# Two attention-and-MLP layers on one core: the last four x tiles of layer 0 turned through device memory, and the k/q weight stores moved behind the loop

## The chip, the core and the metric

The kernel runs on 1 core of a Trainium2 chip. The metric is the device time of one execution in microseconds (us). The kernel before has a median of 1320.75 us in 3 runs (1319.97 to 1321.23).

## What is computed

Two layers are applied to `x` (2048 rows, 640 columns, fp32). Each layer is a linear attention block followed by a squared-ReLU MLP, each with a layer norm ahead of it and a residual around it. Both layers use the same weights.

```python
def _A_ref(x, wqkv, wo):                     # H = 32 heads of Dh = 20
    q, k, v = split_heads(x @ wqkv)
    phi = lambda t: where(t > 0, t + 1, exp(t)) + 1e-6
    pq, pk = phi(q), phi(k)
    kv = einsum("bhsd,bhse->bhde", pk, v)
    z  = einsum("bhsd->bhd", pk)
    o  = einsum("bhqd,bhde->bhqe", pq, kv) / (einsum("bhqd,bhd->bhq", pq, z)[..., None] + 1e-6)
    return merge_heads(o) @ wo

def _B_ref(x, w1, b1, w2, b2):               # F = 1728
    r = maximum(x @ w1 + b1, 0)
    return (r * r) @ w2 + b2

x = x + _A_ref(layernorm(x), wqkv, wo)       # these two lines
x = x + _B_ref(layernorm(x), w1, b1, w2, b2) # are done twice
```

## The kernel before

**Arithmetic.** Every fp32 product is made of three matmuls of a rounded kind: an operand is split into a high part (a ScalarE copy) and a low part (a VectorE subtraction), and the products low-high, high-low and high-high are added up. Each operand that TensorE reads therefore costs one ScalarE copy and one VectorE subtraction.

**Stages of a layer.** First the attention loop over 16 tiles of 128 rows: `part` (line 489 in the profile) projects a tile onto k and q, `Phi` (lines 591, 598, 599) makes exp, min and max of it, and `g_part`/`gt_part` (line 489 too) add up the products of phi(k) with the normalised x. Then a transition (lines 990 to 1170: `late_q`, `kv_make`, `m_make`, `b_out`), which folds v and the output weights into one 640x640 matrix M and finishes the first four tiles of the attention. Then the MLP over four groups of four tiles (lines 1204 and 1287), with the attention's output of the next group woven in (line 489).

**The order of the work** is written out by hand; no scheduler moves an instruction. Each engine runs its own instructions in that order, and stops where an operand is not ready. All loads and stores but two kinds are issued by SyncE's queue (SP), in order too; a DMA there also waits until the one eight places before it has landed. GpSimd (POOL) issues the accumulating stores of `acc` and the stores of `spread_out`.

**One turn of the attention loop, at tile t** (`late` is the set of tiles whose q part is put off to the transition; 11 to 15 are late in layer 0):

- TensorE: first half of `part(t)`, then, for a late tile, at once the second half, then `g_part(t - 1)` and, at every second tile, `gt_part`.
- ScalarE: `exp` of the first half; the high part of `xh`; a high copy of a weight being prepared (`prep.high`, line 301, layer 0 only); the high part of `xT[t + 1]` (line 502); a further `prep.high`; `exp` of the second half; the high part of `kh` (line 783).
- VectorE: the normalisation of `xt[t + 2]` (`a_apply`, line 389), the rest of phi of the first half (598, 599), `prep.low` (313), the rest of phi of the second half, the low part of `xT[t + 1]` (line 505), that of `xh`, statistics of tile t + 3, the low part of `kh`.

**Turning x.** TensorE needs the normalised tile transposed. Both layers do it without TensorE:

- Layer 0, by block moves: VectorE transposes 32x32 blocks inside the tile (`blocks_x`, line 461, in `x_begin(t + 2)` right behind `a_apply`), then ScalarE moves the 16 blocks to their places (`turn_move`, line 475, issued by `move`, 16 small copies a tile).
- Layer 1, through memory: POOL stores the tile to device memory (`spread_out`, line 417), SP reads it back with the blocks spread in four DMAs (`spread_in`, line 426), both in `x_begin(t + 2)`, and VectorE transposes the blocks (`turn`, line 436) in `x_end(t + 1)`, one turn of the loop later, right ahead of the high copy of `xT[t + 1]`.

```python
def x_begin(t):
    yza[t] = blocks_x(xt[t]) if layer == 0 else spread(xt[t])
def x_end(t):
    return yza.pop(t)[1] if layer == 0 else turn(yza.pop(t), True)
```

**Keeping weights.** Layer 0 prepares the split weights of the MLP during its attention loop (`Prep`: loads, `mix` on POOL, `high`, `low`, `store`, lines 246 to 327) and stores them to device memory. The split k/q weights, five tiles `kq[c]` of two halves, are stored too (`keep_kq`, line 196: 640 KB a half), since layer 1 loads them again. Before the change `keep_kq` stands at the start of the turns t = 11 to 15, two halves a turn.

Of the kernel before, what the change touches and what calls it, by code (L numbers as in the profile page):

```python
# [16 lines left out]
NT = S // P  # L17
DC = D // P
# [25 lines left out]

PREP = {1: "aa", 2: "aa", 3: "t", 4: "aa", 5: "t", 6: "aa", 7: "t", 8: "aa", 9: "t", 10: "aa", 11: "t", 12: "aa"}
LATE_T = (5, 6)
PREP_AT = range(1, 14)
N_WARM = 25

# [16 lines left out]
def kernel(  # L66
# [25 lines left out]
    def bank(i, n=1):  # L92
        return PS[:, 512 * i : 512 * (i + n)]
# [17 lines left out]
    def ftile(name):  # L111
        return tmp.tile([P, D], F32, tag="f", name=name, bufs=F_BUFS)
# [82 lines left out]
    def keep_kq(c, j):  # L195
        nc.sync.dma_start(kept["kq", c][:, j], kq[c][:, j].bitcast(F32))
# [215 lines left out]
    def spread_out(src):  # L412

        n = bounce[0] % 8
        bounce[0] += 1
        d = dram.tile([P, D], F32, name="xb", tag=f"xb_{n}")
        nc.gpsimd.dma_start(d, src)
        return d

    def spread(src):  # L420
        return spread_in(spread_out(src))

    def spread_in(d):
        z = ftile("z")
        for j in range(JQ):
            nc.sync.dma_start(
                z[j * B32 : (j + 1) * B32].rearrange("p (i f) -> p i f", f=Q),
                d[:, j * Q : (j + 1) * Q].rearrange("(i q) f -> q i f", q=B32),
            )
        return z  # L430

    def turn(z, strided=False):

        y = ftile("y")
        order = "p (i q c) -> p i c q" if strided else "p (i c q) -> p i c q"
        nc.vector.transpose(
            out=y.rearrange("p (c i q) -> p i c q", c=DC, q=B32),
            in_=z.rearrange(order, c=DC, q=B32),
        )
        return y  # L440
# [18 lines left out]
    def blocks_x(src):  # L459
        y = ftile("y")  # L460
        nc.vector.transpose(
            out=y.rearrange("p (j c q) -> p j c q", c=DC, q=B32),
            in_=src.rearrange("p (j q c) -> p j c q", c=DC, q=B32),
        )
        return [y]

    def turn_move(yz, js):

        if len(yz) == 1:
            yz.append(ftile("z"))  # L470
        yv = yz[0].rearrange("p (j c q) -> p j c q", c=DC, q=B32)
        zv = yz[1].rearrange("p (c i q) -> p c i q", c=DC, q=B32)
        for j in js:
            for i in range(P // B32):
                nc.scalar.activation(  # L475
                    zv[j * B32 : (j + 1) * B32, :, i, :], yv[i * B32 : (i + 1) * B32, j], AF.Copy
                )
# [33 lines left out]
    def proj(ps, aT, w, cs=range(DC)):  # L511

        for c in cs:
            for k, l in ((1, 0), (0, 0), (0, 1)):
                for j in range(2):
                    nc.tensor.matmul(  # L516
                        ps[:, j * 512 : j * 512 + HD], aT[:, k, c, :], w[c][:, l, j * HD : (j + 1) * HD],
                        start=c == 0 and (k, l) == (1, 0), stop=c == DC - 1 and (k, l) == (0, 1),
                    )
# [6 lines left out]
    xt, xT = {}, {}  # L526
# [21 lines left out]
    for layer in range(N_LAYERS):  # L548
# [21 lines left out]
        def xbank():  # L570
            xbanks.append(xbanks.pop(0))
            return bank(xbanks[-1])

        def part(t, a, b, ps=None):

            ps = (xbank() if ps is None else ps)[:, : b - a]
            for c in range(DC):
                mm3(
                    ps, xT[t][:, 0, c, :], xT[t][:, 1, c, :],
                    kq[c][:, 0, a:b], kq[c][:, 1, a:b], c == 0, c == DC - 1,  # L580
                )
            return ps
# [31 lines left out]
        def g_part(t, i):  # L614

            ps = bank(GB[i])
            a, b = xh[t][:, :, i * P : (i + 1) * P], kh[t][:, :, :DM]
            mm3(ps, a[:, 0], a[:, 1], b[:, 0], b[:, 1], t == 0, t == NT - 1)

        def gt_part(p, j, ps):  # L620

            ps, rs = ps[:, :HD], slice(j * HD, (j + 1) * HD)
            for t in (2 * p, 2 * p + 1):
                a, b = kh[t][:, :, DM:], xh[t][:, :, rs]
                mm3(ps, a[:, 0], a[:, 1], b[:, 0], b[:, 1], t % 2 == 0, t % 2 == 1)
            if p == 0:
                nc.vector.tensor_copy(GT_[:, rs], ps)
            else:
                nc.vector.tensor_tensor(out=GT_[:, rs], in0=ps, in1=GT_[:, rs], op=ALU.add)
# [56 lines left out]
        yza = {}  # L686
# [25 lines left out]
        def x1_at(t):  # L712
            g, i = divmod(t, TG)
            if g % 2 == 0:
                return gtile("x1")
            return x1_odd["tile"][:, i]

        def b_load_x(t):
            xr[t] = x1_at(t)
            nc.sync.dma_start(xr[t], src[t])  # L720
# [73 lines left out]

        moved = {}

        def x_begin(t):
            yza[t] = blocks_x(xt[t]) if layer == 0 else spread(xt[t])

        def x_end(t):  # L800
            return yza.pop(t)[1] if layer == 0 else turn(yza.pop(t), True)

        def move(t, n=JQ):

            if layer == 0 and t in yza:
                turn_move(yza[t], range(moved.get(t, 0), n))
                moved[t] = n

        def prep_step(t, i):
            if layer == 0 and t in PREP_AT:  # L810
                if i == 0:
                    prep.mix()
                    prep.load(PREP.get(t + 1, ""))
                prep.low()
                if (t, i) != (1, 0):
                    prep.high()
                if i % 2 == 0:
                    prep.store(2)
# [4 lines left out]
        for t in range(NT):  # L823
# [5 lines left out]
            if layer == 0:  # L829
                if t >= 14:  # L830
                    prep.store()
                if t >= NT - DC:
                    for j in range(2):
                        keep_kq(t - NT + DC, j)
            if t >= 13:
                b_load_pq(t - 13)
                load_vo(2 * t - 26)
# [130 lines left out]
        def late_q(n=1, rest=True):  # L968

            for _ in range(n):  # L970
                if not late_parts:
                    return
                t, j = late_parts.pop(0)
                if j == 0:
                    late_phi[t] = Phi(ftile("rl"))
                late_phi[t].exp(j * HD, part(t, D + j * HD, D + (j + 1) * HD))
                late_todo.append((t, j))
                if rest:
                    late_rest()
# [3 lines left out]
        def late_rest(n=9):  # L983
            for _ in range(min(n, len(late_todo))):
                t, j = late_todo.pop(0)
                late_phi[t].rest()
                if j == 1:
                    nc.sync.dma_start(pqd[t], late_phi.pop(t).r)

        late_q(2)  # L990
        zbc = tmp.tile([P, D], F32, tag="z", name="zbc", bufs=1)
        psz = [xbank()[:, :HD] for _ in range(2)]
# [5 lines left out]
        for i in range(DC):  # L998
            g_part(NT - 1, i)
            nc.scalar.activation(G[:, i], bank(GB[i]), AF.Copy)  # L1000
        for j in range(2):
            gt_part(NT // 2 - 1, j, xbank())
        b_blocks(0)
# [14 lines left out]
        def run_side(n=1):  # L1018
            for _ in range(min(n, len(side_work))):
                side_work.pop(0)()  # L1020
# [48 lines left out]
        def m_split(m):  # L1069
            nc.vector.tensor_copy(M[m][:, 0], m_raw[m])  # L1070
            nc.vector.tensor_tensor(
                out=M[m][:, 1], in0=m_raw[m], in1=M[m][:, 0].bitcast(F32), op=ALU.subtract
            )
# [50 lines left out]

        po = {}

        for i in range(2):
            po[i] = bank(4 + 2 * i, 2)
            proj(po[i], pT[i], M, range(3))
            if i == 0:  # L1130
                m_split(4)
            run_side(2)

        def x_turned(i):

            b_x1(i, po[i])
            yzx[i] = blocks_T(xn.pop(i))
            side_work.extend(lambda k=k: turn_move(yzx[i], (k,)) for k in range(JQ))
            side_work.append(lambda: f_split(i, yzx.pop(i)[1]))

        for i in range(2):
            proj(po[i], pT.pop(i), M, range(3, DC))
            run_side(1)
            b_load_x(i + 2)
        x_turned(0)
        run_side(2)
        x_turned(1)
# [183 lines left out]
        def at(g, n, f):  # L1331
            events.setdefault((g, n), []).append(f)
# [99 lines left out]
        def prep_last():  # L1432
            x1 = x1_odd["tile"]
            h = [R[:, i, 1].rearrange("p c n -> p (c n)")[:, HT + D * j : HT + D * (j + 1)] for i in range(2) for j in range(2)]
            spots = {5: (x1[:, 2], x1[:, 3], h[0]), 6: (h[1], h[3], h[2])}
            for i, p in enumerate(LATE_T):
                at(0, i, lambda p=p: prep.mixes.append(prep.load_t(p, spots[p])))
                at(0, 1 + 3 * i, prep.mix)
            assert len(LATE_T) == len(prep.t)

# [104 lines left out]
```

## Time and profile before

| | |
|---|---|
| median of 3 runs | 1320.75 us (1319.97 to 1321.23) |
| the profiled execution, its own time | 1320.5 us |
| its span, first to last instruction | 1318.5 us |
| TensorE busy | 1310.7 us, 99% |
| VectorE busy | 865.5 us, 66% |
| ScalarE busy | 735.5 us, 56% |
| GpSimd busy | 219.1 us, 17% |
| attention loop of layer 0, transition | to 194 us, 194 to 255 us |
| attention loop of layer 1 | about 663 to 845 us |
| `turn_move`, all | 272 moves, 334 ns each |
| `kept_kq` stores | 10, 640 KB each |

Times in the views are microseconds from the start of the span. PE is TensorE, DVE is VectorE, ACT is ScalarE, SPq and POOLq are the DMA issues of these queues. A row of a timeline has start, duration, engine, line and operation, output<-input with shapes, and the count of like instructions merged into it; brackets at its end name the idle time before it and what ended it.

### The profile page before, as it was taken

To read this page: it belongs to the slowest core of one execution; us is meant where nothing else is said; L and a number is where in the kernel's file an instruction comes from. 1 tells how busy PE (TensorE), PEld (TensorE's weight loads), DVE (VectorE), ACT (ScalarE), POOL (GpSimd) and SP (SyncE) were. 2 spreads that over 40 slices of the span, in tenths; PEclk is the share of its full clock that TensorE was granted. 3 is DMA by queue.
4 is the path that set the end of the run, shared out by engine and by line. 5 is a ranking of instruction groups with operands and counts; after the bars stand their busy time and mean duration, and the time that the engine had idled before them with its cause. 6 is when DMAs were issued, how large, how long until landed. Compare 5 with 4: busy or idle time off the path is not lost.

```text
span 1318.5 us, 20882 instructions
## 1 busy us (share of the span) xinstructions
PE 1310.7 (99%) x7477; PEld 1193.5 (91%) x7477; DVE 865.5 (66%) x1575; ACT 735.5 (56%) x1594; POOL 219.1 (17%) x289
## 2 busy tenths in 40 slices
PE   9999999999999999999999999999999999999998
PEld 8888889989988988998988889999899899889888
DVE  7888958767944954833856677686577559449045
ACT  5888967785475467334322233387844744854242
POOL 2333310064012002101012222001320120120000
PEclk9999999999999999999999999999999999999999
DMA  6898994499974985898954456454869659749756
GB/s 194 247 278 270 336 339 144 152 353 388 320 290 154 302 298 171 267 361 290 361 158 126 123 145 169 124 199 171 315 214 345 212 192 320 290 149 297 286 186 219
DMA packets 135036, 321.57 MB, mean 244 GB/s; under 512 B 16710, under 2 KB 61894, under 8 KB 134294
## 3 DMA queue, kind: packets, MB, share of 16 engines
q1 hardware_dynamic: 127702, 297.96, 67.1%
q0 software_dynamic: 7232, 22.29, 6.4%
q8 instruction: 59, 0.97, 0.3%
q14 instruction: 43, 0.35, 0.1%
HBM read 242.82 MB, written 65.54 MB: 234 GB/s over the span
## 4 chain that ended last, share of the span: by engine, by line
PE 91%; ACT 2%; DVE 2%; DMA 2%; SPq 1%; issue 1%; POOL 0%; ACTq 0%; DVEq 0%; POOLq 0%
PE PS L489 32%; PE PS L1204 28%; PE PS L1287 25%; PE PS L516 3%; ACT z L475 1%; PE PS L1042 1%; PE PS L1055 1%; DMA kq<-kept_kq 1%; SPq L246 1%; PE PS L849 0%; PE PS L637 0%; DMA xt<-in_A_x_dram 0%; DMA kept<-uprep 0%; DVE xT L505 0%; DVE r L599 0%
## 5 line engine op out<-in xcount | busy, mean ns | idle before, releaser
L1204 PE MATMUL PS<-xTb,u 128*128 128x512 f32 x1640 | 376.6, 389 | 0.0
L1204 PEld LDWEIGHTS PS<-xTb,u 128*128 128x128 f32 x1640 | 306.8, 188 | 62.5
L489 PE MATMUL PS<-kq,xT 128*128 128x320 f32 (+2 forms) x1575 | 285.0, 334 | 1.6 <-DVE xT L505 1.4
L489 PEld LDWEIGHTS PS<-kq,xT 128*128 128x128 f32 x1575 | 250.2, 188 | 29.8 <-DVE xT L505 2.2
L1287 PE MATMUL PS<-u,arena 128*128 128x320 f32 x1644 | 250.2, 309 | 0.0
L1287 PEld LDWEIGHTS PS<-u,arena 128*128 128x128 f32 x1644 | 243.4, 188 | 0.0
L1268 DVE TENSOR_TENSOR arena<-R,arena 128x512 fp32r<-128x512 f32 (+1 forms) x200 | 140.8, 707 | 135.3 <-ACT arena L1259 134.8
L1259 ACT ACTIVATE arena<-R 128x512 fp32r<-128x512 f32 (+1 forms) x200 | 117.9, 593 | 157.9 <-PE PS L1287 131.9
L455 ACT ACTIVATE z<-y 32x160 f32<-32x160 f32 x512 | 171.1, 334 | 49.8 <-DVE y L446 42.2
L1215 ACT ACTIVATE R<-PS,b1sb 128x512 f32<-128x512 f32 x104 | 71.5, 687 | 127.8 <-PE PS L1204 126.9
L489 PE MATMUL PS<-kh,xh 128*128 128x512 f32 x480 | 124.8, 393 | 1.0 <-DVE kh L793 0.9
L383 POOL TENSOR_SCALAR rs<-mv 128x1 f32<-128x1 f32 x64 | 34.9, 546 | 513.8 <-DVE mv L381 513.8
L489 PE MATMUL PS<-uM,pTs 128*128 128x320 f32 x720 | 109.4, 309 | 0.0
L489 PEld LDWEIGHTS PS<-uM,pTs 128*128 128x128 f32 x720 | 107.5, 188 | 1.9
L1287 PE MATMUL PS<-uw,arena 128*128 128x320 f32 x660 | 106.1, 309 | 0.0
L489 PEld LDWEIGHTS PS<-kh,xh 128*128 128x128 f32 x480 | 87.1, 188 | 16.9 <-DVE kh L793 1.8
L1287 PEld LDWEIGHTS PS<-uw,arena 128*128 128x128 f32 x660 | 99.2, 188 | 0.4 <-DVE x L1301 0.2
L1233 DVE TENSOR_TENSOR R<-R 128x512 f32<-128x512 f32 (+1 forms) x128 | 79.5, 626 | 26.0 <-ACT R L1216 26.0
L475 ACT ACTIVATE z<-y 32x160 f32<-32x160 f32 x272 | 90.9, 334 | 3.3
L591 ACT ACTIVATE r<-PS 128x512 f32<-128x512 f32 (+1 forms) x64 | 27.7, 434 | 99.4 <-PE PS L489 98.1
L1216 ACT ACTIVATE R<-R 128x512 f32<-128x512 f32 x104 | 65.8, 633 | 3.3
L598 DVE TENSOR_SCALAR r<-r 128x512 f32<-128x512 f32 (+1 forms) x64 | 21.3, 332 | 70.4 <-ACT r L591 70.2
(135 smaller groups left out, 1318.1 us busy)
## 6 DMA issues: line engine op xcount, KB each, us to landing
u<-kept SPq DMA_DIRECT2D x113, 640.0 KB, 5.6
u<-kept_w SPq DMA_DIRECT2D x104, 640.0 KB, 6.2
u<-kept SPq DMA_DIRECT2D x56, 320.0 KB, 6.1
kept<-uprep SPq DMA_DIRECT2D x49, 320.0 KB, 5.6
z<-xb SPq DMA_DIRECT2D x160, 80.0 KB, 5.3
pqt<-pq SPq DMA_DIRECT2D x32, 320.0 KB, 6.7
acc<-r POOLq DMA_DIRECT2D x28, 320.0 KB, 4.9
uw<-kept SPq DMA_DIRECT2D x14, 640.0 KB, 7.4
```

What stands on the lines that cost most here:

```text
L383: nc.gpsimd.tensor_scalar(rs, mv[:, 1:2], LN_EPS, None, op0=ALU.add)
L455: nc.scalar.activation(zv[j * B32 : (j + 1) * B32, :, i, :], yv[i * B32 : (i + 1) * B32, :, j, :], AF.Copy)
L475: nc.scalar.activation(zv[j * B32 : (j + 1) * B32, :, i, :], yv[i * B32 : (i + 1) * B32, j], AF.Copy)
L489: nc.tensor.matmul(ps, a, b, start=first and i == 0, stop=last and i == 2)
L516: nc.tensor.matmul(ps[:, j * 512 : j * 512 + HD], aT[:, k, c, :], w[c][:, l, j * HD : (j + 1) * HD], start=c == 0 and (k, l) == (1, 0), st ...
L1204: nc.tensor.matmul(ps, a[:, d, :], bb[:, d, :], start=(d, i) == order[0], stop=(d, i) == order[-1],)
L1215: nc.scalar.activation(r, v, AF.Relu, bias=b1sb[:, c : c + 1])
L1216: nc.scalar.activation(r, r, AF.Square)
L1233: nc.vector.tensor_tensor(out=quad(*out, k), in0=quad(*x, k), in1=quad(*y, k), op=op)
L1259: nc.scalar.activation(u[:, 0], v, AF.Copy)
L1268: nc.vector.tensor_tensor(out=u[:, 1], in0=v, in1=u[:, 0].bitcast(F32), op=ALU.subtract)
L1287: nc.tensor.matmul(ps, x, y, start=opens and k == 0 and p == 0 and e == 0, stop=k == PAIRS - 1 and p == b - a - 1 and e == len(seq) - 1, s ...
```

## The change

Tiles 12 to 15 of layer 0 take layer 1's way through memory: their `x_begin` is `spread` and their `x_end` is `turn`. Their block transposes (four, line 461) and block moves (4 x 16, line 475) are gone. The ten `keep_kq` stores leave the loop: two stand ahead of the first `late_q` of the transition, three in the loop over `g_part` of the last tile, five around the first `proj` calls.

```diff
+SPREAD_FROM = 12
 ...
+        def by_moves(t):
+            return layer == 0 and t < SPREAD_FROM
         def x_begin(t):
-            yza[t] = blocks_x(xt[t]) if layer == 0 else spread(xt[t])
+            yza[t] = blocks_x(xt[t]) if by_moves(t) else spread(xt[t])
         def x_end(t):
-            return yza.pop(t)[1] if layer == 0 else turn(yza.pop(t), True)
+            return yza.pop(t)[1] if by_moves(t) else turn(yza.pop(t), True)
         def move(t, n=JQ):
-            if layer == 0 and t in yza:
+            if by_moves(t) and t in yza:
                 turn_move(yza[t], range(moved.get(t, 0), n))
                 moved[t] = n
 ...
-                if t >= NT - DC:
-                    for j in range(2):
-                        keep_kq(t - NT + DC, j)
 ...
+        keeps = [(c, j) for c in range(DC) for j in range(2)] if layer == 0 else []
+        def run_keep(n):
+            for _ in range(min(n, len(keeps))):
+                keep_kq(*keeps.pop(0))
+        run_keep(2)
         late_q(2)
 ...
         for i in range(DC):
             g_part(NT - 1, i)
             nc.scalar.activation(G[:, i], bank(GB[i]), AF.Copy)
+            if i % 2 == 0:
+                run_keep(1)
 ...
+        run_keep(2)
         for i in range(2):
             po[i] = bank(4 + 2 * i, 2)
             proj(po[i], pT[i], M, range(3))
 ...
             proj(po[i], pT.pop(i), M, range(3, DC))
             run_side(1)
             b_load_x(i + 2)
+            run_keep(2)
```

## The prediction

> **What bounds the kernel now.** I read the page first, then TensorE's timeline over the stretch that the change touches, then the timelines of ScalarE and VectorE there, then the same tiles in layer 1, which already work as the changed ones will.
>
> ```profile
> span 1318.5 us, 20882 instructions
> PE 1310.7 (99%) x7477; PEld 1193.5 (91%) x7477; DVE 865.5 (66%) x1575; ACT 735.5 (56%) x1594; POOL 219.1 (17%) x289
> ```
>
> TensorE is busy 99% of the span and the change leaves its matmuls alone. Time can be won only where TensorE waits, and lost only where a new wait reaches it. The profiled execution took 1320.5 us, 2.0 more than its span; the median of the runs, 1320.75, is 0.25 higher. Sums below are made on the 1320.5 and moved up by that 0.25 at the end. A measurement of this kernel can tell about 0.2%, 2.64 us, from no change.
>
> TensorE's timeline, tiles 12, 13 and 14 of layer 0 (a late tile opens with 30 matmuls of 320 columns):
>
> ```profile
> 152.47 4.56 PE L489 MATMUL PS<-kq,xT 128*128 128x320 f32 x30
> ...
> 162.23 0.38 PE L489 MATMUL PS<-kq,xT 128*128 128x320 f32 x1
> 162.87 4.51 PE L489 MATMUL PS<-kq,xT 128*128 128x320 f32 x29 [0.26 <-DVE xT L505]
> ...
> 170.65 0.30 PE L489 MATMUL PS<-kq,xT 128*128 128x320 f32 x1
> 172.13 4.52 PE L489 MATMUL PS<-kq,xT 128*128 128x320 f32 x29 [1.18 <-DVE xT L505]
> ```
>
> The first matmul of a tile needs only the high part of xT, the second needs the low part, which VectorE makes (L505). Unhindered, one such matmul follows the next by 4.56 / 30 = 0.15 us, as tile 12's do. Tile 13's second comes 0.64 after its first, tile 14's 1.48 after. So 0.49 + 1.33 = 1.8 us are lost here. That is all that a better supply of x could win in this loop.
>
> Why the low parts are late, from ScalarE's timeline:
>
> ```profile
> 147.09 0.44 ACT L591 ACTIVATE r<-PS 128x320 f32<-128x320 f32 x1
> ...
> 149.46 0.72 ACT L301 ACTIVATE uprep<-wq 128x640 fp32r<-128x640 f32 x1
> 150.09 0.42 ACT L591 ACTIVATE r<-PS 128x320 f32<-128x320 f32 x1
> ...
> 152.51 5.52 ACT L475 ACTIVATE z<-y 32x160 f32<-32x160 f32 x16
> 158.06 0.44 ACT L591 ACTIVATE r<-PS 128x320 f32<-128x320 f32 x1
> ...
> 160.42 0.46 ACT L301 ACTIVATE uprep<-st 128x320 fp32r<-128x320 f32 x1
> 160.78 0.42 ACT L591 ACTIVATE r<-PS 128x320 f32<-128x320 f32 x1
> ```
>
> Sixteen block moves hold ScalarE for 5.52 us, and tile 12's first exp starts at 158.06, long after its matmuls. These moves go: 4 x 5.52 = 22 us of ScalarE. But VectorE has next to no room there either:
>
> ```profile
> 147.60 1.41 DVE L461 STREAM_TRANSPOSE y<-xt 128x640 f32<-128x640 f32 x1
> 148.93 0.52 DVE L598 TENSOR_SCALAR r<-r 128x320 f32<-128x320 f32 x1
> 149.49 0.49 DVE L599 SCALAR_TENSOR_TENSOR r<-PS,r 128x320 f32<-128x320 f32 x1
> ...
> 151.39 1.02 DVE L505 TENSOR_TENSOR xT<-z,xT 128x640 fp32r<-128x640 f32 x1
> ...
> 156.81 0.61 DVE L389 TENSOR_SCALAR xt<-xt,mv,rs 128x640 f32<-128x640 f32 x1
> ...
> 162.00 0.81 DVE L505 TENSOR_TENSOR xT<-z,xT 128x640 fp32r<-128x640 f32 x1
> ...
> 167.25 0.61 DVE L389 TENSOR_SCALAR xt<-xt,mv,rs 128x640 f32<-128x640 f32 x1 [0.77 <-POOL rs L384]
> ...
> 171.26 0.81 DVE L505 TENSOR_TENSOR xT<-z,xT 128x640 fp32r<-128x640 f32 x1
> ```
>
> **The turn (the term of the sum).** VectorE loses a block transpose and gains a turn of the same length, so its load is unchanged; what changes is the place. The block transpose stood two tiles ahead, behind `a_apply`. The turn stands behind the rest of the first half's phi, and ScalarE's xT copy must now wait for it, the second exp for that copy, the rest of phi for that exp, and the low part for that. Layer 1's tiles 13 and 14 show this chain with nothing else in it:
>
> ```profile
> 815.69 4.56 PE L489 MATMUL PS<-kq,xT 128*128 128x320 f32 x30
> 823.52 4.56 PE L489 MATMUL PS<-kq,xT 128*128 128x320 f32 x30
> ```
> ```profile
> 818.09 0.44 ACT L591 ACTIVATE r<-PS 128x320 f32<-128x320 f32 x1 [4.08 <-PE PS L489]
> ```
> ```profile
> 818.56 0.33 DVE L598 TENSOR_SCALAR r<-r 128x320 f32<-128x320 f32 x1 [1.21 <-ACT r L591]
> 819.33 1.39 DVE L436 STREAM_TRANSPOSE y<-z 128x640 f32<-128x640 f32 x1
> 822.62 0.82 DVE L505 TENSOR_TENSOR xT<-y,xT 128x640 fp32r<-128x640 f32 x1
> ```
>
> From the turn's start to the end of the low part it takes 822.62 + 0.82 - 819.33 = 4.11 us. From TensorE's start to the end of the low part it takes 823.44 - 815.69 = 7.75, and TensorE is back after 7.83. Layer 1 hides the chain with 0.1 us to spare. Layer 0 has preparation work on the same engines, so here it cannot all be hidden. Tile by tile, with z in time:
>
> - Tile 12. With the block transpose gone, the rest of phi starts at 147.60 and takes 149.98 - 148.93 = 1.05 (the exp of 147.09 is done by 147.53). Turn at 148.65, plus 4.11, plus the weight copy that stands between the xT copy and the exp (150.09 - 149.46 = 0.63): low part done at 153.39. TensorE's second matmul was due at 152.62. It waits 0.77.
> - Tile 13. The low part was done at 152.41, now at 153.39; VectorE works without a break behind it, so `a_apply` moves from 156.81 to 157.79 and ends at 158.40. The rest of phi takes 819.33 - 818.56 = 0.77, the turn starts at 159.17, and 4.11 plus a half weight copy (160.78 - 160.42 = 0.36) later, at 163.64, the low part is done. TensorE arrives at 153.39 + (162.23 - 152.62) = 163.00. The second matmul comes at 163.64 instead of 162.87, 0.77 late.
> - Tile 14. Low part 162.81 before, 163.64 now, so `a_apply` moves by 0.83 from 167.25 to 168.08 and ends at 168.69; rest of phi to 169.46; 4.11 more is 173.57. TensorE arrives at 163.64 + (170.65 - 162.87) = 171.42 and waits. It resumes at 173.57 instead of 172.13, **1.44 late**.
> - Tile 15. No statistics, no `a_apply`, no weights are left. TensorE needs it at 173.57 + 9.61 = 183.2; the chain from tile 14's start is 173.4 + 7.75 = 181.2. No wait, 2.0 us to spare.
>
> So ScalarE's 22 us buy nothing: the moves' delay was hidden to 1.8 us, and the turn's serial chain puts back that and 1.44 more. The ends of this term are -1.8 (both waits vanish) and 3 x 2.0 - 1.8 = +4.2 (all three wait as long as tile 14); I stay with the chain's own sum.
>
> **The bounce (hidden, with conditions).** Each tile adds a 320 KB store on POOL's queue and four 80 KB reads on SP's. Landing times in layer 1 at tile 15, and of a POOL store and of weight stores in the stretch of the change (160 to 165, 150 to 155):
>
> ```profile
> xb<-xt POOLq DMA_DIRECT2D x1, 320.0 KB, 4.0
> z<-xb SPq DMA_DIRECT2D x4, 80.0 KB, 2.0
> ```
> ```profile
> acc<-r POOLq DMA_DIRECT2D x1, 320.0 KB, 6.8
> ```
> ```profile
> kept_w<-uprep SPq DMA_DIRECT2D x2, 640.0 KB, 4.7
> ```
> ```profile
> 821.76 1.75 SPq L426 DMA_DIRECT2D z<-xb  x4
> ```
> ```profile
> 135.02 0.61 DVE L389 TENSOR_SCALAR xt<-xt,mv,rs 128x640 f32<-128x640 f32 x1
> ```
>
> A round trip is 4.0 + 1.75 + 2.0 = 7.75, or 10.6 with the loop's 6.8. Tile 12's store can go when its `a_apply` ends, at 135.63, 13.0 ahead of its turn. Tile 14's can go at 158.4 and its z is needed at 169.5, 11.1 later; tile 15's at 168.7 and, with its 2.0 to spare, 179.1, 10.4 later. Tile 13's can go only after POOL's mixing of weights:
>
> ```profile
> 148.38 0.89 POOL L269 TENSOR_TENSOR wa<-wq,wa 128x320 f32<-128x320 f32 x1
> ```
>
> that is at 149.27, and z is needed at 159.17, 9.9 later. All four are hidden at 7.75; at 10.6 tile 13's would come 0.7 late and tile 15's 0.2. I take 4.0 for the store, because the k/q stores that filled the queues here are gone; 6.8 is kept for the first rival.
>
> The Trainium skill's page "DMA: Bandwidth & Descriptors", section "Anatomy of one DMA — SWDGE (gpsimd) path", gives 2.0 us plus bytes / 436e3 for one DMA: 2.75 us for this store by estimate. The rows here, 4.0 and 6.8, are longer; by the page alone the store would land inside the 4.2 from which the first rival, below, decides, and its chance would be nought. The same page, "Latency and other measured facts", speaks against the change: HBM access takes 0.2 us on average but 2 us at high load, and each tile now makes that trip twice.
>
> **The k/q stores (nothing).** 10 x 640 KB leave the loop, whose DMA engines were full, for the transition, whose engines have gaps:
>
> ```profile
> 210.00:215.00 5.00, 5.00 (x26) 4.13 (x26) 4.75 (x11) 2.03 (x6) 0.00 (x0) 1.00 0.10 39
> 240.00:245.00 5.00, 5.00 (x36) 5.00 (x35) 2.82 (x4) 4.84 (x15) 0.79 (x2) 1.00 0.02 3
> ```
> ```profile
> 228.38 1.19 SPq L720 DMA_DIRECT2D x<-in_A_x_dram  x2
> ```
> ```profile
> 244.38 0.82 DVE L764 TENSOR_TENSOR x<-PS,x 128x640 f32<-128x640 f32 x1
> ```
>
> DMA shares (the column before the last) are 0.10 and 0.02 there. The first five land before the small stores of M are issued; the last five are queued on SP among the first w1 chunks and the two x loads of 228.38. The first user behind them is VectorE, which adds tile 2's x at 244.38, 16 us later. The page's row of rates has full slices at 339 GB/s:
>
> ```profile
> GB/s 194 247 278 270 336 339 144 152 353 388 320 290 154 302 298 171 267 361 290 361 158 126 123 145 169 124 199 171 315 214 345 212 192 320 290 149 297 286 186 219
> ```
>
> Three w1 chunks (640 KB each) and two of the five halves stand ahead of that x: 3.6 MB with it, 10.7 us at 339 GB/s. Even behind all five it would be 5.6 MB, 16.5 us, and half a us late. So I take 0 of the two ends 0 and +0.5. In the loop the stores' leaving frees no TensorE wait by itself, since none of them ended on a DMA.
>
> **Sum:** 1320.5 + 1.44 = 1321.9; on the runs' scale **1322.2 us**.
>
> **Rivals.**
>
> 1. *SP's queue stops behind tile 13's bounce* (slower). SP stands in order: the z reads wait for tile 13's store to land, and behind them is the store of a prepared weight (`kept_w`) whose landing frees the buffer that tile 12's first weight copy on ScalarE needs; that copy stands ahead of tile 13's xT copy. With X the store's landing time, the buffer is free at 149.27 + X + 1.75 + 4.7 = 155.7 + X; it must be by 159.17 + 1.39 - 0.63 = 159.9. It decides from X = 4.2. At X = 6.8 tile 13 is 2.6 later, and tile 14's chain, which starts from there, too: 1322.2 + 2.6 = 1324.8. For: 4.0 is close to 4.2. Against: the k/q stores among the traffic are gone, and 4.7 was measured beside them.
> 2. *The waits go*. If VectorE caught up with the turns, -1.8: 1320.75 - 1.8 = 1318.95, inside 0.2%. For: both waits follow ScalarE's moves in time. Against: 147.60 to 153 leaves VectorE no gap for an earlier turn, and the order of the built program has the turn behind the first half's phi in all four tiles.
> 3. *More is won than TensorE waits.* No row shows where; 1317 or less.
>
> **How the numbers follow.** My forecast 0.57, the first rival 0.28, the second 0.11, the third 0.04. The forecast and the second rival lie within 0.2% (1318.1 to 1323.4); the first rival is slower by more, with its small cases making up for the forecast's upper tail. Faster 0.04, same 0.68, slower 0.28. The range runs from the second rival's 1318.8 to the first one's 1325.0.
>
> **What would show it.** In the changed profile: TensorE's brackets `<-DVE xT L506` at tiles 12, 13 and 14 of about 0.6, 0.3 and 1.9 us; rests of ScalarE ahead of the xT copy, ended by `DVE y`; tile 15 without a wait; the MLP's first matmul some 1.4 us later than before; turns not waiting for z. Turns that wait for `DMA z`, or a weight copy on ScalarE that waits for `kept_w`, speak for the first rival. Tiles 13 and 14 following at 0.15 us would prove the chain wrong, and a wait at the `b_x1` addition the k/q part.

## The result, and the profile after

The changed kernel takes 1325.07 us (median of 6 runs, 1324.18 to 1325.79); the kernel before, run beside it, 1320.02 us (6 runs, 1319.54 to 1321.23). The medians differ by 5.05 us; the ratio is 1.0036, with a 95% interval from 1.0023 to 1.0049, so the change makes the kernel slower by about 0.4%. The profiled execution took 1324.9 us.

The head of the page of the changed kernel (busy time, share of the span, instructions):

```profile
span 1323.2 us, 20853 instructions
...
PE 1311.3 (99%) x7477; PEld 1193.5 (90%) x7477; DVE 864.8 (65%) x1575; ACT 714.6 (54%) x1530; POOL 221.1 (17%) x293
```

ScalarE lost 64 block moves and 21 us, as it should. TensorE has the same 7477 matmuls. Its busy time is 0.6 us longer and the span 4.7, so most of the loss is waiting. The first question is where in the span it arises. The MLP's first matmul in TensorE's timeline, before and after:

```profile
255.36 10.84 PE L1204 MATMUL PS<-xTb,u 128*128 128x512 f32 x47
```
```profile
260.48 5.85 PE L1216 MATMUL PS<-xTb,u 128*128 128x512 f32 x25
```

It comes 5.12 later, and the four matmuls of `acc` that follow tile 15 already come 5.12 later (199.04, before 193.92). So the loss arises in the attention loop, and the transition adds nothing to it. The loop's late tiles in TensorE's timeline after the change:

```profile
153.57 4.52 PE L490 MATMUL PS<-kq,xT 128*128 128x320 f32 x29 [0.90 <-DVE xT L506]
...
164.66 0.38 PE L490 MATMUL PS<-kq,xT 128*128 128x320 f32 x1 [1.34 <-DVE r L600]
165.29 4.52 PE L490 MATMUL PS<-kq,xT 128*128 128x320 f32 x29 [0.26 <-DVE xT L506]
...
173.84 0.41 PE L490 MATMUL PS<-kq,xT 128*128 128x320 f32 x1 [0.60 <-ACT xT L503]
175.78 4.52 PE L490 MATMUL PS<-kq,xT 128*128 128x320 f32 x29 [1.53 <-DVE xT L506]
...
186.23 0.38 PE L490 MATMUL PS<-kq,xT 128*128 128x320 f32 x1 [0.71 <-DVE r L600]
186.87 4.51 PE L490 MATMUL PS<-kq,xT 128*128 128x320 f32 x29 [0.26 <-DVE xT L506]
```

Before, two tiles waited, ahead of their second matmul only. Now all four wait, and tiles 13, 14 and 15 wait ahead of their first matmul too (1.34, 0.60, 0.71). Those are new in kind: the forecast chain behind the turn had none of them, and run 3 below, which has the turn in its new place but no trip, has none. The chain that ended last says where they come from (start, length, what):

```profile
149.09 5.33 DMA xb<-xt
154.43 0.31 SPq L427
...
156.95 0.43 SPq L323
157.42 5.25 DMA kept_w<-uprep
162.83 0.47 ACT uprep L302
...
164.43 0.81 DVE xT L506
...
170.65 5.89 DMA xb<-xt
176.59 0.33 SPq L427
...
178.83 3.75 DMA z<-xb
182.71 1.40 DVE y L437
```

Read from the top: tile 13's store lands 5.33 us after its start; until then SP stands at the first read of z. Behind the four reads stands the store of a prepared weight. Only when that has landed, at 162.7, is the buffer free for ScalarE's second weight copy, behind which the second half's exp of tile 12 waits, and behind that tile 13's low part. That is the path of the first rival. Then the chain goes through memory a second time, in another way: tile 15's store lands after 5.89 us, its reads after another 3.75, and the turn itself waits. (Tile 14's turn waited for z as well, 0.62 us.) ScalarE's row for the first of the two weight copies:

```profile
160.38 0.74 ACT L302 ACTIVATE uprep<-st 128x640 fp32r<-128x640 f32 x1 [3.39 <-DMA kept_w<-uprep]
```

### The profile page after: what moved, and what is told of

It is laid out like the page before. It is cut to its first block, busy times and chain, and to the rows that moved or that the text cites. A ratio compares the mean times of both kernels' runs of the same rounds, so it can differ in the third digit from the quotient of the medians.

```text
span 1323.2 us, 20853 instructions
## 1 busy us (share of the span) xinstructions
PE 1311.3 (99%) x7477; PEld 1193.5 (90%) x7477; DVE 864.8 (65%) x1575; ACT 714.6 (54%) x1530; POOL 221.1 (17%) x293
## 4 chain that ended last, share of the span: by engine, by line
PE 93%; DVE 2%; DMA 2%; SPq 1%; ACT 1%; POOL 1%; issue 0%; DVEq 0%; ACTq 0%; POOLq 0%
PE PS L490 33%; PE PS L1216 28%; PE PS L1299 26%; PE PS L517 3%; PE PS L1052 1%; PE PS L1065 1%; DMA xb<-xt 1%; PE PS L850 0%; PE PS L638 0%; DMA kept<-uprep 0%; DMA kept_w<-uprep 0%; DVE xT L506 0%; DVE bn L380 0%; SPq L427 0%; SPq L247 0%
## 5 line engine op out<-in xcount | busy, mean ns | idle before, releaser
L456 ACT ACTIVATE z<-y 32x160 f32<-32x160 f32 x512 | 171.2, 334 | 49.3 <-DVE y L447 42.3
L476 ACT ACTIVATE z<-y 32x160 f32<-32x160 f32 x208 | 69.5, 334 | 2.6
```

The lines of the kernel that those rows point to most:

```text
L456: nc.scalar.activation(zv[j * B32 : (j + 1) * B32, :, i, :], yv[i * B32 : (i + 1) * B32, :, j, :], AF.Copy)
L476: nc.scalar.activation(zv[j * B32 : (j + 1) * B32, :, i, :], yv[i * B32 : (i + 1) * B32, j], AF.Copy)
```

## The experiments

Two theories stood. *Place*: all of the loss is the turn's place in VectorE's order, a longer chain than forecast. *Trip*: the place costs its forecast 1.44, and the rest is the trip to memory, by SP's hold or by z coming late. To these came the question whether the moved k/q stores cost anything.

**1. The k/q stores alone.**

```
-SPREAD_FROM = 12
+SPREAD_FROM = 16
```

> All 16 tiles of layer 0 turn by ScalarE's block moves, as before; only the ten k/q stores are in the transition. Theory A (all of the +4.3 us comes from the four tiles that go through memory: a round trip of 5.3 to 5.9 us to the z reads, SP's queue held behind them, and VectorE's turn late in its order): 1320.0, within 0.5, and the two waits of before (about 0.5 and 1.3 us ahead of tiles 13 and 14) are still there. Theory B (the k/q traffic in the transition costs): 1320.5 to 1324, with the MLP's first matmul no later than before in the loop but waits behind it. If taking the stores out of the loop is worth something by itself, 1318 to 1319.5.

Measured 1320.03 us beside 1320.23 for the kernel before, ratio 1.0002 (0.9993 to 1.0011). The stores cost nothing in the transition, and their leaving the loop gains nothing by itself. The two waits of before are still there (0.26 and 1.19 us in the brackets of tiles 13 and 14). (Its profiled execution, 1324.34, is not typical: TensorE waited 2.76 us, up to 668.51, for a load of k/q weights in layer 1. The other nine lie between 1319.35 and 1321.17.)

**2. The trip without the k/q move.**

```
+            if layer == 0 and t >= NT - DC:
+                for j in range(2):
+                    keep_kq(t - NT + DC, j)
...
-        keeps = [(c, j) for c in range(DC) for j in range(2)] if layer == 0 else []
+        keeps = []
```

> Tiles 12 to 15 go through memory; the ten k/q stores stay in the loop, two a turn from turn 11, on SP as before. Theory A1 (the loss is the memory round trip and SP's order): with 1.28 MB more a turn beside the trip, the store lands 6 to 9 us after its start instead of 5.3 to 5.9, and z, the buffer that ScalarE's weight copy needs, and tiles 13 to 15 come later by as much: 1326 to 1330. Theory A2 (the loss is the place of the turn in VectorE's order alone): 1325, as with the stores moved. Below 1324 would mean that the k/q move itself costs time.

Measured 1334.36 us, ratio 1.0108 (1.0092 to 1.0125): 9.3 us more than the changed kernel, and beyond the expected range. SP's timeline, the reads of z for tiles 13, 14 and 15:

```profile
156.22 1.85 SPq L427 DMA_DIRECT2D z<-xb  x4
...
168.69 4.18 SPq L427 DMA_DIRECT2D z<-xb  x4
...
181.89 3.49 SPq L427 DMA_DIRECT2D z<-xb  x4
```

The stores had started at 148.98, 158.81 and 171.79 on GpSimd, so the reads begin 7.2, 9.9 and 10.1 us later; in the changed kernel it was 5.3, 5.9 and 5.9. It is not the tile's own store that became so much longer, as was expected: the three landed after 6.3, 5.9 and 4.0 us. SP was still issuing the DMAs ahead of the reads, the k/q stores among them, until 0.1 us before each of these rows starts. So the two halves of the change are not independent: the k/q move is worth nothing alone and 9.3 us beside the trip. A part of the rise is a slower TensorE, which shows in its windows (stretch, length, busy time and matmuls, granted clock, share of the DMA engines, GB/s):

```profile
165.00:167.50 2.50, 1.45 (x5) 0.82 1.01 422
167.50:170.00 2.50, 2.50 (x11) 0.50 1.07 352
...
180.00:182.50 2.50, 2.39 (x9) 0.55 0.98 288
```

The granted clock fell to 0.50 behind waits of 2.57 and 2.26 us; 29 matmuls took 6.05 us instead of 4.52 in these two tiles, and 5.82 in a third, behind a wait of 2.40. That is 4.4 of the 9.3 us.

**3. No trip.** VectorE turns the normalised tile itself, which leaves the blocks of tiles 12 to 15 unmoved.

```
-            yza[t] = blocks_x(xt[t]) if by_moves(t) else spread(xt[t])
+            yza[t] = blocks_x(xt[t]) if by_moves(t) else xt[t] if layer == 0 else spread(xt[t])
```

> As the changed kernel, but tiles 12 to 15 make no trip to memory: VectorE's 32x32 turn reads the normalised tile directly, so the blocks of these tiles are not moved to their places and their projections are of other data. The turn's place in VectorE's order, its 1.4 us, ScalarE's copies, and the k/q stores in the transition are those of the changed kernel. Theory A1 (trip and SP's order): the waits <-DMA kept_w and <-DMA z are gone, tiles 12, 13 and 14 wait about 1.0, 0.3 and 1.9 us, tile 15 none: 1321.5, within 0.7. Theory A2 (place of the turn alone): 1325. If neither the place nor the trip costs, 1320 or less.

Measured 1321.54 us, ratio 1.0010 (1.0001 to 1.0019): 1.3 us over the kernel before, beside a forecast of 1.44 for the place. TensorE's timeline:

```profile
153.46 4.52 PE L490 MATMUL PS<-kq,xT 128*128 128x320 f32 x29 [0.90 <-DVE xT L506]
...
163.57 4.52 PE L490 MATMUL PS<-kq,xT 128*128 128x320 f32 x29 [0.24 <-DVE xT L506]
...
173.35 4.51 PE L490 MATMUL PS<-kq,xT 128*128 128x320 f32 x29 [1.53 <-DVE xT L506]
```

Forecast were 153.39, 163.64 and 173.57, and no wait at tile 15; there is none. *Place* as the whole cause is refuted, and the remaining 3.5 us go with the trip.

**4. The reads of z behind the other stores.**

```
         def x_begin(t):
+            if layer == 0 and not by_moves(t):
+                xs[t] = spread_out(xt[t])
+                return
...
             move(t + 2, AHEAD)
+            if t + 2 in xs:
+                yza[t + 2] = spread_in(xs.pop(t + 2))
```

> As the changed kernel, but the four reads of z for tiles 12 to 15 are put on SP's queue at the end of the loop's turn instead of right behind the tile's store, so that the stores of prepared weights and of tokens go ahead of them. Theory A1 with SP's order as the larger part: ScalarE's 3.39 us wait for the store of a prepared weight ahead of tile 13 goes, tile 13 waits 0.2 to 0.4 us instead of 1.5 and 0.5, z comes no earlier for tiles 14 and 15: 1323 to 1324.3. If the order on SP is nothing and the trip alone counts (or the place alone): 1325, within 0.5. If the reads now come later than the store's landing would let them: 1325.5 to 1327.

Measured 1325.97 us (1324.61 in the profiled execution), ratio 1.0040 (1.0025 to 1.0055): no gain. ScalarE's wait for the weight's buffer is gone, but z is now late at every tile. SP's timeline, then VectorE's:

```profile
152.40 1.02 SPq L323 DMA_DIRECT2D kept_w<-uprep  x2
153.86 2.92 SPq L427 DMA_DIRECT2D z<-xb  x4
```
```profile
161.68 1.35 DVE L437 STREAM_TRANSPOSE y<-z 128x640 f32<-128x640 f32 x1 [1.19 <-DMA z<-xb]
```

The reads were issued 0.6 us sooner than in the changed kernel (153.86 against 154.43), but behind 1.28 MB of weights, and the last lands only at 161.7, 4.9 us after the last issue; in the changed kernel the turn could start at 159.21. Changing the order on SP passes the wait from one user to the other. The time lies in the third outcome of the expectation, but not for its reason: tile 13's reads were not issued late, they landed late.

**5. The trip made, and not used.** Store and reads as in the changed kernel; VectorE turns the normalised tile, as in 3.

```
             yza[t] = blocks_x(xt[t]) if by_moves(t) else spread(xt[t])
+            if layer == 0 and not by_moves(t):
+                yza[t] = xt[t]
```

> As the changed kernel, with the store to memory and the four reads of z made for tiles 12 to 15 as before, but VectorE turns the normalised tile and not z, so nothing waits for z (these tiles' blocks are not moved; their projections are of other data). SP still stands behind the store's landing. Without trip and reads the same turn gave 1321.5, with both 1325.1. Theory A1 (SP held is the larger part): ScalarE's wait of about 3.4 us for the prepared weight's store ahead of tile 13 stays, tile 13 is late by 1.5 and 0.5 us, tiles 14 and 15 as without the trip: 1322.8 to 1323.8. Theory A3 (z's own lateness is the whole): the wait for the buffer costs nothing on TensorE, 1321.5 to 1322.

Measured 1321.47 us, ratio 1.0012 (1.0002 to 1.0021): as without the trip. This reading has a limit. ScalarE still waits for the buffer, but tile 13's store had landed sooner than in the changed kernel (SP's timeline, then ScalarE's):

```profile
153.27 1.90 SPq L427 DMA_DIRECT2D z<-xb  x4
```
```profile
159.96 0.74 ACT L302 ACTIVATE uprep<-st 128x640 fp32r<-128x640 f32 x1 [2.78 <-DMA kept_w<-uprep]
```

The store started at 149.28, so X, its landing time, was 4.0 here and 5.3 in the changed kernel, with the same transfers beside it; why it was shorter stays open. (Tiles 14 and 15 had 5.2 and 5.8.) A hold of that length was hidden: the copy started at 159.96, where the prediction had set the limit at 159.9. So it is shown that the hold at X = 4.0 costs nothing. What it costs at 5.3 with z in time was not separated; the chain of the changed kernel alone puts tile 13's loss on it.

**6, 7. Tiles begun a turn earlier**, without and with the turn ahead of the first half's phi.

```
-            a_load(t + 3, src)
+            if layer > 0 or t + 3 < SPREAD_FROM:
+                a_load(t + 3, src)
...
+            if layer == 0 and t + 4 >= SPREAD_FROM:
+                a_load(t + 4, src)
...
+                if layer == 0 and SPREAD_FROM <= t + 3 < NT:
+                    a_apply(t + 3)
+                    xs[t + 3] = spread_out(xt[t + 3])
...
```

> As the changed kernel, but tiles 12 to 15 are loaded, normalised and stored to memory one turn of the loop (about 10 us) earlier; their reads of z stay at their places on SP, so SP finds the store landed. If the loss beyond the 1.3 us of the turn's place is the trip's latency (theory A1, A3): no wait for z and none for the prepared weight's store, 1321.0 to 1322.3. If it is the traffic itself or SP's issue time (2 to 3 us for four reads): 1323.5 to 1325.

> Both: tiles 12 to 15 begun a turn earlier, and the turn ahead of the first half's phi; all data as the reference has them. If latency and the turn's place are the whole of the loss: 1318.8 to 1320.0, faster than the kernel before by up to 0.1%. If z is then needed too early for the reads (1.2 us sooner than in the changed kernel), a wait of up to 1 us a tile: 1321 to 1323.

Measured 1327.41 us, ratio 1.0060 (1.0046 to 1.0074), and 1328.02 us, 1.0065 (1.0052 to 1.0077). A miss, for a reason of the experiment: to keep a buffer free the load of x stood in the middle of the turn, and the statistics now wait for it. VectorE's timeline of the first of the two:

```profile
149.66 0.89 DVE L380 BATCH_NORM_STATS2 bn<-xt 128x6 f32<-128x320 f32 x2 [3.74 <-DMA xt<-in_A_x_dram]
```

TensorE waits 2.67 us behind that, and 3.13 in the other (whose profiled execution, 1331.14, was the slowest of its five; the other four took 1327.90 to 1328.02). In both kernels the turns of tiles 12 to 14 did not wait for z, so an earlier start can cover the trip, though the late load also gave z more time; tile 15's still did wait, 1.80 and 8.19 us. What the earlier start would be worth without the late load stays open.

**8. The turn ahead of phi, without the trip.**

```
+            turned = None
+            if layer == 0 and t + 1 >= SPREAD_FROM and t + 1 in yza:
+                turned = x_end(t + 1)
             f.rest()
...
```

> As the kernel without the trip (tiles 12 to 15 turned from the normalised tile, blocks not moved), and VectorE's turn stands ahead of the first half's phi and no longer behind it. If the place of the turn is what costs 1.3 us: the waits ahead of tiles 12, 13 and 14 (0.90, 0.24 and 1.53 us) fall to 0.3 or less in sum, 1318.8 to 1319.8, the bound of what these four tiles can give. If the 1.4 us only pass to the phi that then stands behind the turn: 1321.0 to 1322.

Measured 1319.25 us, ratio 0.9994 (0.9985 to 1.0003). Of the three waits one of 0.71 us is left, at tile 14:

```profile
171.58 4.51 PE L490 MATMUL PS<-kq,xT 128*128 128x320 f32 x29 [0.71 <-DVE xT L506]
```

So the place did cost what 3 had shown, and this is the bound: with the trip for nothing and the best place found, these four tiles win 0.9 us, which can't be told from nothing.

**9, 10, 11. The running sum on GpSimd**, to take one transfer of three out of GpSimd's queue; then also the store ahead of the mixing of weights; then also the turn ahead of phi.

```
-                if t < NT - 1:
+                if t < (10 if layer == 0 else NT - 1):
                     nc.gpsimd.dma_start(acc, r, accum_op=ALU.add)
```
```
+            if layer == 0 and SPREAD_FROM <= t + 2 < NT:
+                a_apply(t + 2)
+                xs[t + 2] = spread_out(xt[t + 2])
             prep_step(t, 0)
...
```

> As the changed kernel (1325.1), but from turn 10 on the running sum acc is added by GpSimd in SBUF (1.57 us an add) and no longer by an accumulating DMA of 320 KB on GpSimd's queue; that takes one transfer of three that GpSimd's queue and the full DMA engines carry beside the trip. Theory A3 (the trip is late because the DMA engines and its queue are full): the store lands 1 to 2 us sooner than the 5.3 to 5.9 us of the changed kernel, z for tiles 14 and 15 is on time or nearly, 1321.5 to 1323.5. If the other traffic has no part in the trip's length: 1325, within 0.7. If GpSimd's adds hold up its stores or the weights' mixing: 1326 or more.

> As the last, and the store of tiles 12 to 15 (with its normalisation) stands ahead of GpSimd's mixing of weights instead of behind it: tile 13's store starts about 2.8 us sooner, those of the others 0 to 0.3. Theory A3: tile 13 no longer waits for the prepared weight's store (1.34 us in the changed kernel), 1321.3 to 1322.5, what the turn's place alone costs. If tile 13's start has no part: the same as the last run, within 0.5.

> As the last, and the turn ahead of the first half's phi, which without the trip gave 1319.25. If z is there when the turn comes (1.2 us sooner than in the changed kernel): 1319.2 to 1320.2, level with the kernel before. If z is late by 0.5 to 2 us a tile, the wait now stands ahead of phi too: 1321 to 1326.

Measured 1325.62 us (ratio 1.0042, 1.0029 to 1.0056), 1325.47 (1.0038, 1.0025 to 1.0052) and 1324.30 (1.0030, 1.0019 to 1.0041). In the first, tile 13's store did land in 4.0 us and the reads in a median of 2.2 (from 130 to 190 us), though tile 15's store took 6.2; the gain was given back on VectorE. GpSimd's timeline of the first, then VectorE's of the first and of the changed kernel:

```profile
153.55 2.07 POOL L791 TENSOR_TENSOR acc<-acc,r 128x640 f32<-128x640 f32 x1 [0.94 <-DVE r L600]
```
```profile
154.12 2.18 DVE L929 TENSOR_TENSOR xh<-xt,xh 128x640 fp32r<-128x640 f32 x1
```
```profile
153.44 0.82 DVE L929 TENSOR_TENSOR xh<-xt,xh 128x640 fp32r<-128x640 f32 x1
```

The subtraction that met GpSimd's add took 2.18 us instead of 0.82, and everything behind it moved: the next turn started at 161.26, 2.05 later than in the changed kernel, without waiting for z. (0.68 of that was there when the subtraction started, the other 1.37 is its own.) Only the third outcome of the first expectation, an add that holds up other work, was near it, and it named the wrong engine. The second run came out as its expectation had it for a start of tile 13 that plays no part; but the store started only 1.7 us sooner than in the first and took 5.2 to land, so that part is hardly tested. The third lies in its second outcome, where z is late: tile 15's turn waits 3.42 us for it.

**12. The sum left out.** To take the traffic away and put no work elsewhere, `acc` isn't updated in turns 10 to 14.

```
-                if t < NT - 1:
+                if layer == 0 and 10 <= t < NT - 1:
+                    pass
+                elif t < NT - 1:
                     nc.gpsimd.dma_start(acc, r, accum_op=ALU.add)
```

> As the changed kernel (1325.1), but the sum acc is not updated in turns 10 to 14 at all: neither by the accumulating DMA nor by GpSimd (five terms of the denominator are left out). Only traffic is taken away beside the trip, 320 KB a turn on GpSimd's queue, with no work put on another engine. Theory A3 (trip and SP's hold are long because queue and DMA engines are full): the store lands about 4 us after its start, z's reads in about 2.2 us as in the run with the sum on GpSimd, no wait for z and no late weight buffer; what is left is the turn's place: 1321.3 to 1322.5. If the remaining traffic fills the engines all the same: 1323 to 1325.

Measured 1321.56 us, ratio 1.0013 (1.0004 to 1.0023): the same as without a trip (1321.54), and TensorE has the same three waits (0.93, 0.26, 1.52). Tile 13's second matmul, at 165.29 in the changed kernel, starts here at:

```profile
163.60 4.52 PE L490 MATMUL PS<-kq,xT 128*128 128x320 f32 x29 [0.26 <-DVE xT L506]
```

DMA issues from 148 to 177 us, with the median from issue to landing, of the changed kernel and of this one:

```profile
xb<-xt POOLq DMA_DIRECT2D x3, 320.0 KB, 5.9
acc<-r POOLq DMA_DIRECT2D x3, 320.0 KB, 6.0
z<-xb SPq DMA_DIRECT2D x10, 80.0 KB, 3.7
```
```profile
xb<-xt POOLq DMA_DIRECT2D x3, 320.0 KB, 5.3
z<-xb SPq DMA_DIRECT2D x12, 80.0 KB, 3.3
```

The trip shrank less than expected: X was 4.8, 5.3 and 5.3 at tiles 13 to 15, not 4, where the changed kernel had 5.3, 5.9 and 5.9; SP's four reads took 1.75 us to issue instead of 2.5 to 3.2. That was enough. The first weight copy on ScalarE waits till 158.87 instead of 160.38, the second not at all, tile 14's turn doesn't wait for z, and tile 15's 2.06 us for z stay inside the room that this tile has. With the accumulating transfers and their issue on GpSimd gone, the changed kernel loses its 3.5 us, though the trip is only 1.3 to 2 us shorter up to SP's release: it stood at the edge of what the loop hides. Which part of the trip they lengthen is less clear. X was 4.0, 5.2 and 5.8 in run 5, where they were made, and 3.9, 4.7 and 6.2 in run 9, where they were not, so it is not shown that the store's own landing time comes from them. No run leaves the sum out without the trip, either; but the three waits that are left here are those of run 3, which has the sum.

## Why the prediction was right or wrong

- **Where time can be won.** No run speaks against it: 1.8 us of waits were taken for all, and the best run, 8, wins 0.9 us, which can't be told from nothing.
- **The turn's place, +1.44.** Right in size and in every tile: run 3 gives +1.3 (interval 0.1 to 2.5), the second matmuls within 0.22 us of the forecast times, and no wait at tile 15.
- **The k/q stores, 0.** Right for the stores alone (run 1). Not seen was their worth to the other half of the change: without the move the trip would have cost 9.3 us more (run 2).
- **The bounce, hidden.** This step failed. The store was taken at 4.0 us, from a tile of layer 1, "because the k/q stores that filled the queues here are gone"; it measured 5.3, 5.9 and 5.9. The reads were taken at 1.75 to issue and 2.0 to land; they measured 2.5 to 3.2, and 3.7 in the median. A trip of 7.75 became 5.33 + 2.52 to SP's release at tile 13, and 5.89 + 2.29 + 3.75 = 11.9 at tile 15, against 10.4 of cover. The row for this stretch had been shown, 6.8 for GpSimd's other store, and was set aside for a row of a quieter one. (That other store took 6.8 us in layer 1 too, beside the 4.0, so its row alone did not say how much longer the trip's store would be.) What lengthened the trip past its cover were the transfers of that other store, with their issue (run 12); how much of it was the store's landing and how much SP's reads behind it stays open. The Trainium skill's page "DMA: Bandwidth & Descriptors", section "Anatomy of one DMA — SWDGE (gpsimd) path", would have 2.75 us for the trip's store by estimate; the trace says twice that, and the trace decides.
- **The first rival.** It named the path, and 1324.8 against 1325.07 measured looks like its price too, but that is in part luck. Its 2.6 us were for X = 6.8 and for the hold at tile 13 alone; by its own sum the measured X of 5.3 gives 1.1. Against run 3, tile 13's second matmul comes 1.7 us late (165.29 against 163.57), tile 14's 2.4 and tile 15's 3.8 (186.87 against 182.93 + 0.15). So by the rows about half of the loss beyond the turn's place is the hold, and the buffer that decided there was the second weight's; the rest, at tiles 14 and 15, is z's own lateness, which the rival did not have. Its point of decision fits the runs: at X = 4.0 the hold was hidden (run 5), at 5.3 the chain of the changed kernel runs through it.
- **The time.** The result is 2.9 us over the forecast and 0.07 past the upper end of the range. Against the kernel before as run beside it (1320.02, where the forecast started from 1320.75) the loss is 5.05 us where 1.44 was forecast, so 3.6 were missed.
- **The other rivals.** The waits did not go, and no run won time outside of TensorE's waits.

No version was found that beats both kernels. The k/q move alone is level with the kernel before; the best of those that turn tiles through memory and leave nothing out, run 11, is 0.3% slower.

## What to carry to other kernels

Cost a new transfer by the rows of the stretch it will run in, and by the queue it will stand in, not by the same transfer where the engines are quieter: here a trip 1.3 to 2 us shorter was hidden (run 12), and the longer one cost 3.5 us. When a load waits for a store on an in-order queue, look for what stands behind it there and whose buffer that frees. And before work is moved off an engine, add up the waits on the engine that bounds the kernel: the 22 us of ScalarE's moves cost TensorE at most 1.8 us, and the shortest way to that bound is a run with the new path's cost taken away (run 8: 0.9 us).

## What the runs showed of the hardware

- GpSimd's add and VectorE's two-input subtraction hardly ran side by side (run 9): the subtraction took 2.18 us instead of 0.82 and ended 0.7 after GpSimd's add did, and the add took 2.07 where the kernel before has 1.57 for the same add at tile 15. The Trainium skill's page "SBUF — State Buffer", section "SBUF: two separate sides", has the two engines share a port pair as an exclusive lock when a VectorE instruction with two SBUF inputs meets a GpSimd one that reads SBUF; the trace agrees. It made a 2 us add on an otherwise idle engine as dear as the transfer that it replaced (1325.62 against 1325.07 us).
- Behind single waits of 2.26 to 2.57 us TensorE's granted clock was 0.50 for about 3.4 us (run 2, in windows of 0.5 us), and it fell to 0.50 behind waits of 2.67 (run 6) and 2.76 us (the profiled execution of run 1) as well. Waits of up to 1.70 us (run 4) left it at 1.00. Between these no run has a wait. A late tile can so cost more than its wait.
